# Attention and two feed-forward layers on one core: inverse norm spread by one-pass products, narrower strided scores, and a re-planned order

## The chip, the cores and the metric

The kernel runs on one core of one Trainium2 chip. TensorE, VectorE, ScalarE, GpSimd (POOL in the profile) and SyncE work side by side, each through its own instruction stream, and wait for one another by semaphores; SyncE issues the DMA transfers. The metric is the device time of one execution in microseconds. Before the change the median of three runs is 887.65 us.

## What is computed

Attention over 4 batches, 8 heads, 576 positions and a head width of 64: the first four heads see a local window of 32 positions, the last four every 32nd position. The result, 2304 tokens by 512, goes through a gated feed-forward layer with an RMS norm ahead of it, and then through a second layer with a squared ReLU.

```python
mask_local = (rel >= 0) & (rel < stride)
mask_strided = (rel >= 0) & (pos[None, :] % stride == pos[:, None] % stride)
...
scores = np.where(masks[None, :, :, :], scores, -1000000000.0)
...
return np.matmul(attn, v).astype(np.float32)
```

```python
rms = np.sqrt(np.mean(x * x, axis=-1, keepdims=True) + 1e-06)
xn = x / rms * rms_g
g = xn @ w_gate
silu = g * (1.0 / (1.0 + np.exp(-g)))
val = xn @ w_val
return (silu * val @ w_out).astype(np.float32)
```

```python
h = x @ w_in
r = np.maximum(h, 0.0)
g = r * r
return (g @ w_out).astype(np.float32)
```

## The kernel before

**Attention.** There are 16 units, each a batch with a pair of heads; even units are local, odd units strided. A unit goes through a chain of steps: scores (`att_qk`, products of 64 columns at L476), mask and exponentials, sums, a norm (`att_norm`, L545), a turn of the probabilities so that keys lie on partitions, and the attention product `xo` with v (`att_pv`, L612). In a strided unit the 576 positions are sorted into 32 residues of 18 positions, and a score tile takes a group of three residues (`GR` = 54 positions), so that 54 of its 64 columns belong to the group. Units 0 to 6 put their scores into the bank pair `a` (`first_acc`) and units 7 and 8 into rotating banks `s`; in these nine the mask is added ahead by a product with the mask (L464, `masked`), in the others by VectorE (`att_mask`, L490). Units 0 to 6 are turned by TensorE (`att_turn`, L567) and copied to SBUF (`att_keep`, L579). The others are turned in blocks of 32 by VectorE, and eight DMAs (`att_swap`, L593) move the turned pieces to their place, `pt<-tr`.

**Norm.** The tokens are worked in five blocks, of 512 columns but for the last. For each block, square sums are taken by one-column products (`msb`, L900; for block 0 they are `ms`, L660), VectorE adds the epsilon (`inv`, L906), POOL takes the power (L913), and `prep_bc` (L922) spreads the inverse root over 128 partitions: for each chunk of up to 128 tokens an f32 product whose stationary operand is the column of inverses, broadcast to 128 columns, against an identity. VectorE multiplies x by the spread and by g (`xn`, L939), and x is split into a high part (ScalarE, L958 or L960) and a low part (VectorE or POOL, L970 or L975).

**Feed-forward.** Weights and x are split into f32r pairs, and each block product is three f32r products (`mm3`, L1427 to L1429), in the first phase 512 columns wide: the "wide products" below, into the rotating banks `gv` and the accumulators `a`. The later phases work on 384 columns, with sums of blocks made by VectorE (L1960) and products at L1912 and L2318. The first phase and the attention are interleaved up to about 245 us.

**What sets the order.** The order of all instructions on every engine is fixed when the program is built, by a planner: each `Task` is a chain of steps, each step has alternatives (an engine letter, a planned cost and, for TensorE, a count of records), and `advance()` takes, among the steps that could start first by the planned times, within `TOL`, the one with the earliest due time. Due times come from the leads and from `PRI`; `LOADF`, `BIAS` and the `D_` constants choose between engines; `PV_AHEAD` bounds how many units the scores may run ahead of the attention products. While `warming`, gaps of TensorE are filled with products on a blank tile (`fill()`, L2479). DMAs that leave SyncE's queue stand in the same plan: `lanes.dma` gives the planned landing. The planner's times are only its own; on the chip, order and semaphores alone count. The core of the choice:

```python
e = min(found, key=lambda e: min(f[0] for f in found[e]))
first = min(f[0] for f in found[e])
start, due, _, task, a = min((f for f in found[e] if f[0] <= first + tol), key=lambda f: f[1:3])
...
if e == "T" and warming and start - free["T"] > 2 * FILL:
    fill(int(FILL_OF * (start - free["T"]) / FILL))
emit(task, a)
```

## Time and profile before

| | |
|---|---|
| median of 3 runs | 887.65 us (886.38 to 887.7) |
| profiled execution, its own time | 888.92 us |
| span from first to last instruction in it | 887.1 us |
| mean granted TensorE clock | 0.995 |
| TensorE busy | 873.0 us (98%) |
| TensorE weight loads busy | 817.5 us (92%) |
| VectorE busy | 646.2 us (73%) |
| ScalarE busy | 449.0 us (51%) |
| POOL busy | 69.4 us (8%) |

Times in the profile are microseconds from the span's start. A row of the timeline has the start, the time from there to the end of the last of its instructions, the engine, the line of the kernel, the operation, the tile written and those read, their shapes and how many instructions of the kind follow one another; in brackets the engine's idle time before it and what ended it. One f32 product stands as two records, an f32r product as one. Successive products overlap, so the price of a product is the distance from its start to the next one's start. A busy share of 98% says that the order of TensorE's instructions is the time, and that its waits are few; the granted clock of a stretch tells whether the same instructions ran at 2.4 GHz (1.00) or at 1.2 GHz (0.50).

### The profile page before, as it was taken

Reading aid. Unit: us, or ns where it says so; the run is one execution under the profiler, and the core shown is the slowest. Engines: PE = TensorE matmul, PEld = TensorE weight load, DVE = VectorE, ACT = ScalarE, POOL = GpSimd, SP = SyncE. Lnnn points to the kernel's source line nnn. Section 1 sums busy time; section 2 is a strip of 40 time slices with the busy share of each in tenths; the row PEclk is TensorE's granted clock in tenths of the full one; section 3 lists DMA queues with packets and bytes.
Section 4 is the critical chain, followed back from the end, with each engine's and each line's share of the span. In section 5 each row is a group of like instructions: output and inputs, shape, how many; then the busy total and the mean of one; then the engine's idle time right before and its main releaser. Section 6 shows DMA issues by size and latency. Waiting matters only on the chain.

```text
span 887.1 us, 17217 instructions
## 1 busy us (share of the span) xinstructions
PE 873.0 (98%) x6777; PEld 817.5 (92%) x6782; DVE 646.2 (73%) x1098; ACT 449.0 (51%) x1149; POOL 69.4 (8%) x64
## 2 busy tenths in 40 slices
PE   7999999999999999999999999999999999999998
PEld 4778778878888999999999999999999999999998
DVE  5998877977889875956975876868875456548466
ACT  5986786323312243534543546656565375364462
POOL 0110600100100000000100100001000003002002
PEclk9999999999999999999999999999999999999999
DMA  9865563676694996494488999876799989949714
GB/s 341 273 215 188 169 217 82 212 234 219 232 362 174 341 408 248 171 356 173 161 322 328 377 406 350 333 273 234 287 303 328 375 323 377 298 178 352 241 34 181
DMA packets 77585, 236.79 MB, mean 267 GB/s; under 512 B 7488, under 2 KB 29760, under 8 KB 71616
## 3 DMA queue, kind: packets, MB, share of 16 engines
q1 hardware_dynamic: 77504, 235.70, 73.4%
q8 instruction: 53, 0.87, 0.4%
q14 instruction: 28, 0.23, 0.1%
HBM read 151.91 MB, written 80.48 MB: 262 GB/s over the span
## 4 chain that ended last, share of the span: by engine, by line
PE 85%; DMA 8%; DVE 5%; issue 1%; ACT 1%; SPq 0%; DVEq 0%; ACTq 0%
PE a L1912 15%; PE pg L1912 8%; PE pb L1912 7%; PE gv L1427 6%; PE a L1427 6%; PE a L1428 5%; PE a L1429 5%; PE gv L1429 5%; PE gv L1428 5%; PE a L2318 5%; PE pg L2318 3%; DMA wst_a<-in_w 3%; DMA wi_d<-wst_a 2%; PE pb L2318 2%; DMA wf_d<-wst_a 1%; PE xo L612 1%
## 5 line engine op out<-in xcount | busy, mean ns | idle before, releaser
L1912 PE MATMUL a<-ra 128*128 128x384 f32 x912 | 173.1, 335 | 0.6 <-DVE fb L1960 0.6
L1912 PEld LDWEIGHTS a<-ra 128*128 128x128 f32 x912 | 159.7, 188 | 1.4 <-DVE fb L1960 0.9
L1427 PE MATMUL gv<-ra 128*128 128x512 f32 (+1 forms) x240 | 91.5, 381 | 0.0
L1428 PE MATMUL gv<-ra 128*128 128x512 f32 (+1 forms) x240 | 88.8, 370 | 0.0
L1429 PE MATMUL gv<-ra 128*128 128x512 f32 (+1 forms) x240 | 88.8, 370 | 0.0
L1912 PE MATMUL pg<-ra 128*128 128x384 f32 x426 | 83.4, 336 | 0.7 <-DVE fb L1960 0.7
L1912 PE MATMUL pb<-ra 128*128 128x384 f32 x426 | 83.0, 335 | 0.3 <-DVE fb L1960 0.3
L1912 PEld LDWEIGHTS pg<-ra 128*128 128x128 f32 x426 | 74.8, 188 | 1.2 <-DVE fb L1960 1.0
L1912 PEld LDWEIGHTS pb<-ra 128*128 128x128 f32 x426 | 74.8, 188 | 0.6 <-DVE fb L1960 0.6
L1366 DVE TENSOR_TENSOR wst_a<-fa,wst_a 128x512 fp32r<-128x512 f32 (+1 forms) x76 | 47.9, 632 | 21.6 <-ACT wst_a L1330 19.2
L1427 PEld LDWEIGHTS gv<-ra 128*128 128x128 f32 x240 | 45.5, 190 | 7.9
L1429 PEld LDWEIGHTS gv<-ra 128*128 128x128 f32 x240 | 45.5, 190 | 7.9
L1428 PEld LDWEIGHTS gv<-ra 128*128 128x128 f32 x240 | 45.6, 190 | 6.9
L1330 ACT ACTIVATE wst_a<-fa 128x512 fp32r<-128x512 f32 (+1 forms) x60 | 34.5, 577 | 31.0 <-DMA wi_d<-wst_a 18.9
L1429 PE MATMUL a<-ra,rb 128*128 128x384 f32 x144 | 48.4, 336 | 0.0
L1427 PE MATMUL a<-ra,rb 128*128 128x384 f32 x144 | 48.4, 336 | 0.0
L1428 PE MATMUL a<-ra,rb 128*128 128x384 f32 x144 | 48.4, 336 | 0.0
L1427 PE MATMUL a<-ra 128*128 128x512 f32 (+1 forms) x120 | 45.6, 380 | 0.9 <-ACT pt L579 0.9
L1428 PE MATMUL a<-ra 128*128 128x512 f32 (+1 forms) x120 | 44.9, 374 | 0.0
L1429 PE MATMUL a<-ra 128*128 128x512 f32 (+1 forms) x120 | 44.9, 374 | 0.0
L1514 ACT ACTIVATE fa<-gv 128x512 f32<-128x512 f32 (+1 forms) x18 | 9.5, 527 | 65.5 <-PE gv L1429 65.5
L1199 DVE SCALAR_TENSOR_TENSOR fa<-wst_a,fa 128x1024 int32<-128x1024 int32 x34 | 41.6, 1224 | 1.0
(259 smaller groups left out, 1913.7 us busy)
## 6 DMA issues: line engine op xcount, KB each, us to landing
wst_a<-in_w SPq DMA_DIRECT2D x34, 1024.0 KB, 6.0
ra<-wi_d SPq DMA_DIRECT2D x18, 1792.0 KB, 10.2
wi_d<-wst_a SPq DMA_DIRECT2D x42, 512.0 KB, 4.0
rb<-wf_d SPq DMA_DIRECT2D x16, 1024.0 KB, 7.8
xf_d<-ra SPq DMA_DIRECT2D x21, 768.0 KB, 5.0
ra<-xf_d SPq DMA_DIRECT2D x21, 768.0 KB, 7.1
wo_d<-wst_a SPq DMA_DIRECT2D x14, 512.0 KB, 8.4
wf_d<-wst_a SPq DMA_DIRECT2D x28, 256.0 KB, 7.0
```

The costliest lines, as they stand in the source:

```text
L612: nc.tensor.matmul(out=o, lhsT=v, rhs=rhs, start=True, stop=True)
L1199: nc.vector.scalar_tensor_tensor(out=bits(), in0=word(1), scalar=-0x40000000, in1=bits(), op0=ALU.bitwise_and, op1=ALU.bitwise_or)
L1330: nc.scalar.activation(out=dst, in_=by_form(raw(a, b)), func=ACTF.Copy)
L1366: eng.tensor_tensor(out=x[:, :, 1], in0=by_form(raw(a, b)), in1=x[:, :, 0].bitcast(F32), op=ALU.subtract)
L1427: nc.tensor.matmul(out=o, lhsT=whi, rhs=x_hi, start=first, stop=False)
L1428: nc.tensor.matmul(out=o, lhsT=whi, rhs=x_lo, start=False, stop=False)
L1429: nc.tensor.matmul(out=o, lhsT=wlo, rhs=x_hi, start=False, stop=last)
L1514: nc.scalar.activation(out=tile_t()[:, :n], in_=ps[:, :n], func=ACTF.Silu)
L1912: nc.tensor.matmul(out=o, lhsT=l, rhs=v, start=need is None and k + n == 0, stop=k == 1 and n == 2, skip_group_check=need is not None,)
L2318: nc.tensor.matmul(out=c[role, m]["ap"][:, :SN], lhsT=l, rhs=v, start=need is None and first and i == 0, stop=last and i == 2, skip_group_ ...
```

## The change

There are five parts. Constants of the planner are new. `prep_hi` and `prep_lo` split the inverse into an f32r pair `ih`, the high part by ScalarE and the rest by POOL or VectorE, and `prep_bc` spreads it with two f32r products for each chunk in place of one f32 product. Strided scores with a mask product have `GR` = 54 columns. A rule forces a wide product: after the opening, where a step would make the time since the planned end of the last wide product longer than `SMALL_RUN`, a wide product that could start within `WIDE_IN` is taken first. And the planned landing of turned pieces is `PT_LAG` later.

```diff
--- before.py
+++ after.py
@@ -54,15 +54,15 @@
 
 RING = 9
 
-ATT_LEAD, ATT_STEP = 5.322, 0
-PREP_LEAD = 6.258
-W_LEAD = 0
-X_LEAD = 4.164
+ATT_LEAD, ATT_STEP = 6.027, 0
+PREP_LEAD = 7.671
+W_LEAD = 0.644
+X_LEAD = 4.057
 WARM0 = 10
 
 HOP = 0.15
 DRAIN = 0.12
-TOL = 0.152
+TOL = 0.044
 FILL, FILL_OF, T0, W1_AT = 0.215, 0.85, 5.3, 11.631
 NRAW = 2
 
@@ -76,12 +76,12 @@
 N_QK, N_PV = {"loc": 160, "str": 96}, {"loc": 144, "str": 88}
 QK0, PV0 = {"loc": 1.0, "str": 0.9}, {"loc": 1.25, "str": 0.9}
 
-PRI = {"qk": -3.7, "mask": 12.1, "mx": -12.4, "exp": -0.1, "eps": -0.5, "sum": 15.6, "norm": -1.1, "turn": 3.4, "keep": 12.1, "tr": -1.6,
-       "swap": -2, "pv": -2.7, "out": -1.4, "sq": -3, "ms0": 9.4, "add": -1.3}
-MXP, LOADF, BIAS = 8.164, 0.752, 0.972
-
-D_BUSY, D_COST, D_LATE, D_COST2 = 138.427, 1.084, 343.785, 0.648
-PV_AHEAD = 5
+PRI = {"qk": -2, "mask": 15.3, "mx": -8.6, "exp": -3.6, "eps": 8.4, "sum": 19.5, "norm": 18.3, "turn": -7.3, "keep": 8.7, "tr": -3.7,
+       "swap": 6, "pv": -6, "out": 1.1, "sq": -3.7, "ms0": 11, "add": -2.5}
+MXP, LOADF, BIAS = 11.454, 0.807, 0.253
+
+D_BUSY, D_COST, D_LATE, D_COST2 = 158.279, 1.01, 343.785, 0.648
+PV_AHEAD = 8
 
 
 NM = 7
@@ -108,12 +108,13 @@
     ("P1", 0, 0, "A", None), ("P5", 3, 1, "D", None), ("P6", 4, 2, "A", "s1"), ("P2", 1, 3, "C", "s1"),
     ("P7", 5, 4, "A", "u2"), ("P3", 6, 5, "D", "s5"), ("P4", 2, 6, "A", "c22"),
 ]
-W2_LEAD, X2_LEAD, L2_LEAD = 9.442, -0.326, 6.418
+W2_LEAD, X2_LEAD, L2_LEAD = 9.489, -0.326, 6.418
 X3_LEAD, O_LEAD, H_LEAD = 3.503, -1.055, -0.697
 O_ORDER = [(0, 0), (0, 1), (1, 0), (1, 1), (0, 2), (1, 2), (0, 3), (1, 3)]
 O_ORDER += [(3, 0)] + [(2, j) for j in range(4)] + [(3, j) for j in range(1, 4)]
 O_ORDER += [(p, j) for p in range(4, 7) for j in range(4)]
 W3_LEAD, LOADF2, BIAS2, TOL2 = 16.305, 0.334, 1.147, 0
+SMALL_RUN, WIDE_IN, PT_LAG = 8.246, 0.509, 0.8
 X2_PRI = -0.95
 
 
@@ -157,7 +158,7 @@
 
     def __init__(self):
         self.free = {"T": 0.0, "D": 0.0, "A": 0.0, "P": 0.0, "Q": 0.0, "M": 0.0, "port": 0.0}
-        self.given, self.fetched = 0, 0.0
+        self.given, self.fetched, self.wide_end = 0, 0.0, 0.0
 
     def start(self, e, ready):
         start = max(self.free["D" if e == "X" else e], ready)
@@ -353,6 +354,9 @@
     def transfer(due, ready, cols, fn, allowed=None, early_t=None, run=0):
 
         spawn([Task(due, [(allowed, [[("Q", 0.0)]], lambda _, t: fn(lanes.dma(cols, t, run=run)), early_t)])], ready)
+
+    def is_wide(part):
+        return len(part) > 2 and part[1] > 0.08 * part[2] and part[1] > 1.0
 
     def advance():
 
@@ -400,6 +404,13 @@
             start, _, _, task, a = min(near, key=lambda f: f[1:3])
         if e == "T" and warming and start - free["T"] > 2 * FILL:
             fill(int(FILL_OF * (start - free["T"]) / FILL))
+        if e == "T" and not warming and start + 2 * half - lanes.wide_end > SMALL_RUN:
+
+            wide_ones = [f for f in found["T"] if is_wide(f[3].steps[0][1][f[4]][0]) and f[0] < start + WIDE_IN]
+            if wide_ones:
+                start, _, _, task, a = min(wide_ones, key=lambda f: f[:3])
+        if e == "T" and is_wide(task.steps[0][1][a][0]):
+            lanes.wide_end = start + task.steps[0][1][a][0][1]
         emit(task, a)
         return True
 
@@ -465,6 +476,7 @@
                     out=sc[h][:, 0:64 * nt], lhsT=cst_sb[:, 0:128], rhs=mask_of(u), start=True, stop=False
                 )
         m = 32 if kind(u) == "loc" else 64
+        w = GR if masked and m == 64 else 64
         for t in range(nt):
             for i in range(128 // m):
                 if m == 32:
@@ -474,7 +486,7 @@
                 for h in range(2):
                     r = slice(64 * h, 64 * h + 64)
                     nc.tensor.matmul(
-                        out=sc[h][m * i:m * i + m, 64 * t:64 * t + 64], lhsT=qt[r, c:c + m], rhs=kt[r, c:c + 64],
+                        out=sc[h][m * i:m * i + m, 64 * t:64 * t + w], lhsT=qt[r, c:c + m], rhs=kt[r, c:c + w],
                         start=not masked, stop=not masked or t == nt - 1,
                     )
         for h in range(2):
@@ -746,7 +758,7 @@
             take("pt")
             turn("pt")
             att_swap(u)
-            cell["pt"] = lanes.dma(128 * nt, t, 8, 64 * nt)
+            cell["pt"] = lanes.dma(128 * nt, t, 8, 64 * nt) + PT_LAG
             give("tr", cell["pt"])
 
         def turned(_, t):
@@ -822,7 +834,7 @@
         if u < NM:
             steps += [
                 (
-                    lambda: in_turn("qk", u) and (u < 2 or ("sc", u - 2) in done), [[("T", QK0[kd] + 0.5, N_QK[kd] + 4)]], qk,
+                    lambda: in_turn("qk", u) and (u < 2 or ("sc", u - 2) in done), [[("T", QK0[kd] - (0.1 if kd == "str" else 0.0) + 0.5, N_QK[kd] + 4)]], qk,
                     lambda: max(done["qk", u], done.get(("sc", u - 2), 5.3)), due - 10 - PRI["qk"],
                 ),
                 (
@@ -834,7 +846,7 @@
             steps.append(step(
                 "qk", lambda: in_turn("qk", u) and order.get("prep", 0) and order.get("pv", 0) >= u - PV_AHEAD
                 and room("s", 2) and room("sm") and in_turn("sm", u),
-                [[("T", QK0[kd] + (0.5 if masked else 0.0), N_QK[kd] + (4 if masked else 0))]], qk,
+                [[("T", QK0[kd] + ((0.5 if kd == "loc" else 0.4) if masked else 0.0), N_QK[kd] + (4 if masked else 0))]], qk,
                 lambda: max(done["qk", u], rel["s"][1], rel["sm"][0] - 2.0),
             ))
             if masked:
@@ -914,15 +926,29 @@
             out=inv[:CH, :m], in0=inv[:CH, :m], in1=half[:CH, 0:1].to_broadcast([CH, m]), op=ALU.pow
         )
 
+    def prep_hi(i):
+        inv = pend[i][1]
+        m = len(chunks(i))
+        pend[i] += (st_p.tile([128, 2, 8], F32R, tag="ih", name="ih"),)
+        nc.scalar.activation(out=pend[i][2][:CH, 0, :m], in_=inv[:CH, :m], func=ACTF.Copy)
+
+    def prep_lo(i, eng):
+        _, inv, two = pend[i]
+        m = len(chunks(i))
+        eng.tensor_tensor(
+            out=two[:CH, 1, :m], in0=inv[:CH, :m], in1=two[:CH, 0, :m].bitcast(F32), op=ALU.subtract
+        )
+
     def prep_bc(i):
-        inv = pend[i][1]
+        _, inv, two = pend[i]
         ps = s_p.tile([128, 512], F32, tag="s", name="bc")
         o = 0
         for e, (_, _, skip, m) in enumerate(chunks(i)):
-            nc.tensor.matmul(
-                out=ps[:, o:o + m], lhsT=inv[:CH, e:e + 1].to_broadcast([CH, 128]), rhs=ident[:CH, skip:skip + m],
-                start=True, stop=True,
-            )
+            for h in range(2):
+                nc.tensor.matmul(
+                    out=ps[:, o:o + m], lhsT=two[:CH, h, e:e + 1].to_broadcast([CH, 128]),
+                    rhs=cst_sb[:CH, skip:skip + m], start=h == 0, stop=h == 1,
+                )
             o += m
         pend[i] = ps, inv
 
@@ -1086,8 +1112,10 @@
             ),
             (None, [[("D", 0.2)]], inv, None),
         ]) + [
-            (None, [[("P", 1.1)]], pw, None),
-            (lambda: room("s"), [[("T", 0.25 * nch, 4 * nch)]], bc, lambda: rel["s"][0]),
+            (None, [[("P", 1.25)]], pw, None),
+            (None, [[("A", 0.22)]], lambda _, t: prep_hi(i), None),
+            (None, [[("P", 0.25)], [("X", 0.2)]], lambda p, t: prep_lo(i, nc.gpsimd if p[0][0] == "P" else nc.vector), None),
+            (lambda: room("s"), [[("T", 0.14 * nch, 4 * nch)]], bc, lambda: rel["s"][0]),
         ] + ([(None, [dve(n, True), act(n, True)], keep, None)] if i == 0 else [])))
 
 
```

The order changes from the opening to the end of attention; the tail of TensorE's stream, some 3,700 products, stands in the same order. Three places follow. On TensorE at the square sums and the spread of block 1 (`msb` square sums, `sc` scores of a unit, `bc` the spread, `gv` wide products) the order before is:

```order
L1429 MATMUL gv<-ra 128x512
L900 MATMUL msb<-ones,ssq 128x1 x5
L476 MATMUL sc<-fa 64x64 x24
L922 MATMUL bc<-cst_sb,inv 128x64
L922 MATMUL bc<-cst_sb,inv 128x128 x3
L922 MATMUL bc<-cst_sb,inv 128x64
L1427 MATMUL gv<-ra 128x512
```

and now:

```order
L1457 MATMUL a_1278<-ra 128x512
L912 MATMUL msb<-ones,ssq 128x1 x5
L1455 MATMUL gv<-ra 128x512
...
L488 MATMUL sc<-fa 32x64 x40
L1455 MATMUL gv<-ra 128x512
...
L948 MATMUL bc<-cst_sb,ih 128x64 x2
L948 MATMUL bc<-cst_sb,ih 128x128 x6
L948 MATMUL bc<-cst_sb,ih 128x64 x2
```

Twelve wide products now stand between the square sums and a local score, and twelve more between that and the spread, whose ten products stand in place of five.

On TensorE in the opening, from the turn of unit 3 (`a_179<-cst_sb,sm`) to the turn of unit 4 (`a_178<-cst_sb,sm`), the order before is (`ms` the first block's square sums, `xo` an attention product):

```order
L567 MATMUL a_179<-cst_sb,sm 64x64 x24
L660 MATMUL ms_182<-ones,sq 128x1 x4
L612 MATMUL xo<-pt,v 64x64 x22
L464 MATMUL a_179<-cst_sb 128x384 x2
L476 MATMUL a_179<-fa 64x64 x24
L1427 MATMUL gv<-ra 128x512
...
L922 MATMUL bc<-cst_sb,inv 128x128 x4
L567 MATMUL a_178<-cst_sb,sm 64x64 x20
```

and now, from the attention product of unit 3 to the first wide product behind that of unit 4 and the spread:

```order
L624 MATMUL xo<-pt,v 64x64 x22
L475 MATMUL a_179<-cst_sb 128x384 x2
L488 MATMUL a_179<-fa 64x54 x24
L579 MATMUL a_178<-cst_sb,sm 64x64 x20
L672 MATMUL ms_182<-ones,sq 128x1 x4
L475 MATMUL a_178<-cst_sb 128x320 x2
L488 MATMUL a_178<-fa 32x64 x40
L624 MATMUL xo<-pt,v 64x32 x36
L1455 MATMUL gv<-ra 128x512
...
L948 MATMUL bc<-cst_sb,ih 128x128 x8
```

The wide products that stood between these steps now stand ahead of the turn of unit 3 and behind the attention product of unit 4; the fillers ahead of the first product into a bank `a` of the feed-forward layer are 59 in place of 47.

On SyncE, from the weight stores ahead of unit 14's turned pieces (`pt<-tr 32x320`) to those of unit 15 (`pt<-tr 32x384`, the second), the order before is (`wst` loads of weights, `wi_d` stores of split weights, `yp_d` a 1 MB store of block results, `v` a load):

```order
L1357 DMA wi_d_128<-wst_a 256x1x512
L1140 DMA wst_a<-in_w 128x2x1024
L1357 DMA wi_d_128<-wst_a 256x1x512
L1607 DMA yp_d<-fa 512x1x512
L439 DMA v<-in_strd 128x768
L1357 DMA wi_d_128<-wst_a 256x1x512
L593 DMA pt<-tr 32x320 x8
L1357 DMA wi_d_128<-wst_a 256x1x256
```

and now:

```order
L1385 DMA wi_d_128<-wst_a 256x1x512 x2
L605 DMA pt<-tr 32x320 x8
L1635 DMA yp_d<-fa 512x1x512
L1385 DMA wi_d_128<-wst_a 256x1x512
L1385 DMA wi_d_128<-wst_a 256x1x256
L450 DMA v<-in_strd 128x768
L1168 DMA wst_a<-in_w 128x2x1024
L605 DMA pt<-tr 32x384 x8
```

The store of `yp_d` has moved from ahead of unit 14's pieces to behind them, and so stands between them and unit 15's.

## Rows read from the trace of the kernel before

**Rows 1.** The page's part 1: busy time of each engine.

```profile
PE 873.0 (98%) x6777; PEld 817.5 (92%) x6782; DVE 646.2 (73%) x1098; ACT 449.0 (51%) x1149; POOL 69.4 (8%) x64
```

**Rows 2.** What TensorE waited for, whole span: total us, times, longest.

```profile
PE xo L612 <- issue: 2.9, 1, 2.9
...
PE pg L1912 <- DVE fb L1960: 0.7, 1, 0.7
```

**Rows 3.** Two stretches by engine: length, busy us, granted clock, DMA share, GB/s.

```profile
104.10:107.50 3.40, 3.40 (x13) 3.01 (x13) 3.05 (x9) 3.35 (x20) 3.40 (x5) 0.50 1.02 410
...
199.65:203.05 3.40, 3.40 (x9) 2.63 (x8) 2.14 (x3) 2.03 (x6) 0.00 (x0) 0.50 0.80 225
```

**Rows 4.** TensorE in time, 89 to 107 us: start, us, instruction [idle <-releaser].

```profile
89.10 0.93 PE L476 MATMUL sc<-fa 64*64 64x64 f32 x48
89.96 0.50 PE L1427 MATMUL gv<-ra 128*128 128x512 f32 x1
...
100.31 0.39 PE L1429 MATMUL gv<-ra 128*128 128x512 f32 x1
100.54 1.17 PE L900 MATMUL msb<-ones,ssq 128*128 128x1 f32 x10
101.64 1.25 PE L476 MATMUL sc<-fa 64*64 64x64 f32 x48
103.65 1.97 PE L922 MATMUL bc<-cst_sb,inv 128*128 128x64 f32 x10 [0.76 <-DVE sm L490]
...
105.96 0.63 PE L1428 MATMUL gv<-ra 128*128 128x512 f32 x1
```

**Rows 5.** TensorE in time: a local unit's attention product, and that of unit 14.

```profile
115.96 1.25 PE L612 MATMUL xo<-pt,v 64*64 64x32 f32 x72
117.14 0.50 PE L1427 MATMUL gv<-ra 128*128 128x512 f32 x1
...
196.82 0.30 PE L612 MATMUL xo<-pt,v 64*64 64x32 f32 x4
...
198.30 1.12 PE L612 MATMUL xo<-pt,v 64*64 64x32 f32 x60 [0.38 <-DMA pt<-tr]
199.35 0.56 PE L1427 MATMUL a<-ra 128*128 128x512 f32 x1
```

**Rows 6.** The norm's small tiles, and TensorE around square sums and spread.

```profile
L922 PEld LDWEIGHTS bc<-cst_sb,inv x40: 185/190/333, 45.1 to 234.6; 128*128 128x128 f32 x40
...
L906 DVE TENSOR_SCALAR inv<-msb x4: 151/158/167, 101.8 to 231.6; 128x5 f32<-128x5 f32 x2, 128x4 f32<-128x4 f32 x1, 128x2 f32<-128x2 f32 x1
...
156.85 0.95 PE L900 MATMUL msb<-ones,ssq 128*128 128x1 f32 x8
157.66 0.48 PE L1427 MATMUL gv<-ra 128*128 128x512 f32 x1
...
222.57 1.22 PE L922 MATMUL bc<-cst_sb,inv 128*128 128x128 f32 x10
223.61 0.47 PE L1427 MATMUL gv<-ra 128*128 128x512 f32 x1
```

**Rows 7.** TensorE in time, the opening: fillers, a turn, scores, the bank a.

```profile
8.34 3.88 PE L2479 MATMUL warm<-blank 128*128 128x512 bf16 x17 [0.16 <-issue]
...
35.94 1.61 PE L567 MATMUL a<-cst_sb,sm 64*64 64x64 f32 x48 [0.28 <-DVE sm L545]
...
41.06 0.56 PE L476 MATMUL a<-fa 64*64 64x64 f32 x19 [0.40 <-issue]
...
62.75 0.50 PE L1427 MATMUL a<-ra 128*128 128x512 f32 x1 [0.87 <-ACT pt L579]
```

**Rows 8.** SyncE's DMA queue around unit 14: start, us to issue, transfer.

```profile
183.36 0.59 SPq L1607 DMA_DIRECT2D yp_d<-fa  x1
185.62 0.33 SPq L439 DMA_DIRECT2D v<-in_strd  x1
...
186.77 10.11 SPq L593 DMA_DIRECT2D pt<-tr  x8
```

## The prediction

> **What bounds the kernel now.** I read the page first: TensorE is busy for 873.0 of 887.1 us [rows 1], so the time is TensorE's instruction stream, plus the few places where that stream pauses, plus the places where it runs at half clock. A faster VectorE or ScalarE is worth nothing by itself. The list of what TensorE waited for comes second, and it is short [rows 2]: the longest entry is 2.9 us of "issue", one wait of an attention product in the opening; behind it nothing is over 0.9 us, and of the stages behind the opening only sums at L1960 stand there, with 0.7. Third come the stretches with their granted clock [rows 3]: two of them, 104.10 to 107.50 and 199.65 to 203.05, ran at a granted clock of 0.50, which is 1.2 GHz of 2.4. At half clock 3.4 us do the work of 1.7, so each fall costs **1.7 us**. What stood ahead of a fall is the fourth view, TensorE's instructions in order. Before the first fall come ten square-sum products of one column, 48 small score records, a wait of 0.76 us on the mask add, and the spread of the norm [rows 4]. Before the second, the attention product of unit 14 stops for turned pieces [rows 5]. Both places are narrow work with a wait in it, and both are followed by wide products that take longer: 0.63 us each where one takes 0.39 at full clock [rows 4].
>
> So what this change can win is counted directly: the two falls, the waits ahead of them, and whatever the narrow instructions themselves become cheaper by.
>
> **Part 1: the spread in two one-pass products.** A 512-column block's spread is 10 or 8 records, each with a load of 128 columns. The trace has 40 loads [rows 6]. The new form has two f32r products for each old f32 product, and the old one already stands as two records in the trace, so 40 records stay 40 records. What sets their distance? Eight square-sum records with one column each go from 156.85 to 157.66, 101 ns each, though they stream nothing; ten spread records with up to 128 columns go from 222.57 to 223.61, 104 ns each [rows 6]. The load, not the columns, sets both. I take **0**. The other end: if the columns set it, one pass is priced by a wide product, 230 ns for 512 columns (100.31 to 100.54) [rows 4], in proportion 57 ns at 128. Then 40 x (104 - 57) = 1.9 us would be won. For each of the five blocks ScalarE gets a copy of the inverse and POOL or VectorE a subtraction, both on a few columns; VectorE's own small step on the inverse takes 0.16 us [rows 6]. They lie between the power and the spread, and there the new order has 12 or more wide products in every block but the first, and scores, a turn and six wide products in that, so they are hidden; without that cover they would cost about 0.3 us a block. The Trainium skill, "TensorE: Matmul & The Clock Gate", section "Back-to-back issue gap", gives 81 ns for a sustained pair of load and product of 128 columns; by it the spread would gain 40 x (104 - 81) = 0.9 us, an estimate from that page. The trace's 101 ns at a single column speak against it.
>
> **Part 2: scores of 54 columns.** Four masked strided units write 54 columns instead of 64. A record's price by its columns: an attention product of 72 records with 32 columns takes 1.18 us until the next (115.96 to 117.14), 16.4 ns each [rows 5]; a strided score of 48 with 64 columns takes 0.86 (89.10 to 89.96), 17.9 ns each [rows 4]. Ten columns fewer are 10/32 of that difference, 0.5 ns; by 48 records and 4 units **-0.1 us** (bounds 0, where only the record counts, and -0.5, where a record's 17.9 ns shrink in proportion: 48 x 4 x 17.9 x 10/64 = 0.54).
>
> **Part 3: the opening.** The order has 59 fillers against 47, all ahead of the first product into the bank `a`. A filler takes 0.22 us (17 in 3.88 us) [rows 7], so 12 add 2.6 us unless they fill waits that are there anyway. What can go: the 0.87 us before the first `a` product (the copy of a turned unit by ScalarE), 0.40 us of issue within a score product, and 0.28 before a turn [rows 7], 1.55 together: in the new order 24 wide products stand between that turn and its neighbour, so its copy is covered. The 2.9 us of issue [rows 2] lie ahead of the place where the orders part, and stay. I take 2.6 - 1.55 = **+1.1 us** (bounds -1.5, where fillers only fill waits, and +2.6).
>
> **Part 4: the two falls and their waits.** In block 1 the new order puts 12 wide products, one local score and 12 wide products between square sums and spread. The spread no longer queues on a score bank that the mask has yet to empty, and no narrow stretch is left there. Gone: 1.7 us of clock, and the score's time until the next, 2.01 us (101.64 to 103.65) where the same kind of score takes 0.86 [rows 4], so 1.15. At unit 14 the pieces go out ahead of the 1 MB store of yp instead of behind it: in the trace that store is issued at 183.36 and SP's next issue comes at 185.62, 2.3 us later, while the eight pieces follow at 186.77 and take until 196.88 to be issued [rows 8]. Their planned landing is also 0.8 later. Gone: 1.7 us of clock, and the attention product's 2.53 us (196.82 to 199.35) fall to 1.18 [rows 5], so 1.35. Sum **-5.9 us**.
>
> **Part 5: what comes in their place.** Every step between 63 and 245 us stands somewhere else. I can follow the order, not the waits that it makes. Three places are doubtful: unit 15's pieces are now the ones behind the store, two weight stores and a load; POOL takes some 15 more instructions than before, splits above all; and the new stretch without wide products in the opening (rival 2). The old order lost 5.9 us in the same stretch, in two places. I take half of it, **+2.95 us**; bounds 0 and 5.9. After 245 us the order is the same up to the choice of buffers, so the waits on VectorE's sums at L1960 [rows 2] stay, and cost nothing more or less.
>
> **Sum.** 0 - 0.1 + 1.1 - 5.9 + 2.95 = -1.95 us. The profiled execution took 888.92 us, 1.27 above the median of 887.65 of the runs. 888.92 - 1.95 = 887.0 for a profiled run; **885.7** against the median.
>
> **The rivals.**
> *1. Nothing gained.* New waits of some 5 us in place of 2.95, one of them a fall of 1.7 behind another narrow stretch, bring back all that the repair won: 885.7 + 2.05 is 887.7. For it speaks that the rule that forces a wide product acts by planned times, and the old order, planned in the same way, had them. Against it, that both places are visibly repaired in the order.
> *2. Slower.* The new opening has one stretch with no wide product between the attention products of units 3 and 4: attention, mask, scores, turn, sums, mask, scores, attention, some 250 records in about 7 us by the same steps in the trace of before. In the old opening such a run of small records ended in 2.9 us of issue [rows 2], and two narrow stretches were followed by a fall of 1.7. If both strike, 2.9 + 1.7 = 4.6 us come on top: 890.3. It decides from 3.7 us on, where 885.7 passes 889.4. Against it: behind that one wait the longest for issue in the opening is the 0.40 us of part 3.
> *3. The spread becomes cheap.* The columns set the price and 1.9 us are won: 883.8. For it: the one-pass form isn't in the trace at this width, and all 40 spread records in it are of the f32 form; against it, the 101 ns of records with one column. The page of the Trainium skill that part 1 names has a figure between.
> *4. A clean order.* New waits of about 0.5 us in place of 2.95, and both falls gone: 885.7 - 2.45 is 883.2.
>
> **How the numbers follow.** A measurement of this kernel tells about 0.2%, 1.8 us, from no change: faster is under 885.9, slower over 889.4. My forecast (new waits of 1.5 to 4.3 us, so 884.2 to 887.0) gets 0.40, of which 0.25 is faster and 0.15 the same; rival 1 gets 0.20 (0.18 same, 0.02 slower); rival 2 gets 0.14 (0.13 slower, 0.01 same); rival 3 gets 0.10 and rival 4 gets 0.16, all faster but 0.01. Together 0.50 faster, 0.35 same, 0.15 slower. The range 881.8 to 889.2 leaves out most of rival 2 and the best end of rival 4, where all bounds fall well.
>
> **What would show it.** Right: no stretch after the opening at 0.50 before the end; unit 14's attention product about 1.2 us long with no wait on turned pieces; a spread of about 1.0 us; TensorE's waits between 63 and 245 us of under 3 us together. Wrong: a spread of about 0.6 us (rival 3), a wait of "issue" of over 1 us between 38 and 55 us (rival 2), or a new stretch at 0.50 behind unit 15's attention product or behind a square sum (rival 1). If the first `a` product starts over 3 us later than 62.75, part 3 was priced too low.

## The result and the profile after

The change is **slower**: 896.78 us, the median of four runs (896.26 to 899.72), against 887.67 for the kernel before, measured beside it (886.38 to 887.81). The ratio is 1.0105, with a 95% interval of 1.0085 to 1.0125. The prediction was 885.7 and its range ended at 889.2, so it has the wrong sign. The profiled execution took 899.72 us with a span of 897.89, 10.8 more than the one before [rows 1], so the profile shows the whole loss, and a little more.

The page of after, its busy times and the shares of the chain that ended last:

```profile
PE 876.0 (98%) x6788; PEld 816.9 (91%) x6794; DVE 643.0 (72%) x1079; ACT 457.1 (51%) x1159; POOL 88.8 (10%) x83
...
PE 71%; DMA 15%; DVE 10%; ACT 2%; issue 2%; POOL 0%; SPq 0%; ACTq 0%; DVEq 0%; POOLq 0%
```

TensorE is busy for 3 us more than in [rows 1], POOL for 19 us more. The second line says more than the first: the chain that sets the end now runs on TensorE for only 71% of the time. The same line of the kernel before:

```profile
PE 85%; DMA 8%; DVE 5%; issue 1%; ACT 1%; SPq 0%; DVEq 0%; ACTq 0%
```

The list of what TensorE waited for, after, longest in total first (us in total, times, longest):

```profile
PE xo L624 <- ACT sm L536: 2.3, 2, 1.7
PE xo L624 <- issue: 2.0, 1, 2.0
PE a L1940 <- ACT fa L1966: 1.6, 1, 1.6
PE xo L624 <- DMA pt<-tr: 1.3, 2, 0.8
PE pg L1940 <- DVE fb L1988: 1.3, 2, 0.7
...
PE gv L1456 <- issue: 1.2, 1, 1.2
```

Beside [rows 2] the longest wait on issue is shorter, 2.0 in place of 2.9, but a second one of 1.2 has come. Waits on ScalarE are new: an attention product that waits for a bank which the exponentials still read, and, late in the program, products at L1940 that wait for ScalarE and VectorE.

Where the time went is read off three marks that both traces have: the first product into the bank `a`, the first product of 256 columns (from there on both have the same TensorE instructions in the same order), and the last product.

```
                            before    after
first product into a         62.75    70.28   +7.53
from there to first 256     219.04   216.48   -2.56
from there to the last      601.44   606.78   +5.34
```

The first mark does not hold quite the same work: unit 7's scores stand ahead of it now and stood behind it before. On TensorE they take 1.29 us, after; before, they stood at 69.75 and took 1.30:

```profile
56.01 0.51 PE L475 MATMUL sc<-cst_sb 128*128 128x384 f32 x2
...
57.30 0.50 PE L1455 MATMUL gv<-ra 128*128 128x512 f32 x1
```

So some 6.2 of the 7.53 us are lost in the opening and 1.3 have only moved, and of the 2.56 won behind it 1.3 are those same products.

**The places that the change repaired** look as forecast. The stretches of [rows 3] in the trace of after (length, busy us of PE, PEld, DVE, ACT and POOL, then the granted clock, 1.00 now, DMA share and GB/s), and as a third row the only new one at half clock before the end:

```profile
104.08:107.49 3.41, 3.41 (x18) 2.86 (x18) 3.06 (x9) 2.96 (x10) 2.98 (x4) 1.00 0.30 118
199.65:203.06 3.41, 3.41 (x23) 2.81 (x16) 3.31 (x4) 1.53 (x5) 0.00 (x0) 1.00 1.02 352
...
21.50:28.40 6.90, 6.57 (x122) 5.58 (x119) 5.13 (x6) 4.91 (x23) 1.78 (x1) 0.51 0.80 263
```

The spread of block 1 and the attention product of unit 14, in TensorE's order of time, answer to [rows 4] and [rows 5]:

```profile
103.26 1.20 PE L948 MATMUL bc<-cst_sb,ih 128*128 128x64 f32 x10
104.29 0.47 PE L1455 MATMUL a<-ra 128*128 128x512 f32 x1
...
198.50 1.25 PE L624 MATMUL xo<-pt,v 64*64 64x32 f32 x72
199.68 0.50 PE L1455 MATMUL gv<-ra 128*128 128x512 f32 x1
```

The spread takes 1.03 us to the next product, as in [rows 6] (1.04): one pass saves nothing. Unit 14's product takes 1.18, with no wait. But the wait has come back one unit later. Unit 15's pieces stand behind the store now, and its product stops for them twice, 1.34 us, as much as unit 14's repair was to give (1.35):

```profile
211.72 0.33 PE L624 MATMUL xo<-pt,v 64*64 64x64 f32 x4 [0.84 <-DMA pt<-tr]
212.55 0.81 PE L624 MATMUL xo<-pt,v 64*64 64x64 f32 x40 [0.50 <-DMA pt<-tr]
```

Nor are unit 14's pieces out sooner in this execution. They are issued from 187.50 to 196.82, in [rows 8] from 186.77 to 196.88, and the product comes 1.68 us later than before:

```profile
187.50 9.32 SPq L605 DMA_DIRECT2D pt<-tr  x8
```

**The opening** is where the prediction broke. VectorE's norms of units 3, 5 and 6, before:

```profile
34.93 0.96 DVE L545 TENSOR_TENSOR sm<-sm,ri 128x768 f32<-128x768 f32 x1
...
52.95 0.96 DVE L545 TENSOR_TENSOR sm<-sm,ri 128x768 f32<-128x768 f32 x1
58.60 0.82 DVE L545 TENSOR_TENSOR sm<-sm,ri 128x640 f32<-128x640 f32 x1
```

and after:

```profile
38.60 1.80 DVE L557 TENSOR_TENSOR sm<-sm,ri 128x768 f32<-128x768 f32 x1
...
55.79 0.96 DVE L557 TENSOR_TENSOR sm<-sm,ri 128x768 f32<-128x768 f32 x1
63.78 1.08 DVE L557 TENSOR_TENSOR sm<-sm,ri 128x640 f32<-128x640 f32 x1
```

A norm ends a unit's chain of scores, maximum, exponentials and sums, and TensorE's turn waits for it. The 7.53 us are three steps of this chain: unit 5's norm is 2.84 later (55.79 against 52.95); from it to unit 6's 7.99 pass in place of 5.65, 2.34 more; and from that to the first product into `a` 6.50 in place of 4.15 [rows 7], 2.35 more. Ahead of unit 3's norm, 3.67 late, lies the stretch at half clock from 21.6, half of whose length is 3.4. It is not what makes `a` late: in the run of the change's order with the old forms, below, nothing ahead of `a` is at half clock, and the three steps are 1.52, 2.39 and 2.35, 6.26 together. The second step holds unit 7's scores, ahead of unit 5's turn. What fills the last step is seen on TensorE, after:

```profile
65.42 1.32 PE L579 MATMUL a<-cst_sb,sm 64*64 64x64 f32 x37
...
68.58 0.81 PE L624 MATMUL xo<-pt,v 64*64 64x64 f32 x40 [1.67 <-ACT sm L536]
70.28 0.50 PE L1455 MATMUL a<-ra 128*128 128x512 f32 x1 [0.89 <-ACT pt L591]
```

and on ScalarE in the same microseconds:

```profile
65.70 0.35 ACT L536 ACTIVATE sm<-sc,nm 128x64 f32<-128x64 f32 x1
...
66.81 1.13 ACT L1209 ACTIVATE fa<-wst_a 128x1024 f32<-128x1024 f32 x1
67.85 0.29 ACT L536 ACTIVATE sm<-sc,nm 128x64 f32<-128x64 f32 x1
...
69.46 0.77 ACT L591 ACTIVATE pt<-a 128x320 f32<-128x320 f32 x2
```

The exponentials on `sc` are unit 7's, which the new order gives out before unit 5's attention product and unit 6's copies. They hold the banks that unit 5's product wants (1.67), a step of the weights (1.13) stands among them, and the copy that frees `a` comes only at 69.46, though the turn ended before 67. In the trace of before, unit 7's scores come after the first product into `a`.

### The profile page after: what moved, and what is told of

Its sections match the earlier page's. It is cut to its first block, busy times and chain, and to the rows that moved or that the text cites. A ratio compares the mean times of both kernels' runs of the same rounds, so it can differ in the third digit from the quotient of the medians.

```text
span 897.9 us, 17241 instructions
## 1 busy us (share of the span) xinstructions
PE 876.0 (98%) x6788; PEld 816.9 (91%) x6794; DVE 643.0 (72%) x1079; ACT 457.1 (51%) x1159; POOL 88.8 (10%) x83
## 4 chain that ended last, share of the span: by engine, by line
PE 71%; DMA 15%; DVE 10%; ACT 2%; issue 2%; POOL 0%; SPq 0%; ACTq 0%; DVEq 0%; POOLq 0%
PE a L1940 14%; DMA wi_d<-wst_a 9%; PE pg L1940 8%; PE pb L1940 7%; PE a L2346 5%; PE a L1455 4%; PE a L1456 4%; PE a L1457 4%; DMA wst_a<-in_w 3%; PE pg L2346 3%; PE gv L1455 3%; PE gv L1456 3%; PE gv L1457 3%; DMA wf_d<-wst_a 2%; PE pb L2346 2%
## 5 line engine op out<-in xcount | busy, mean ns | idle before, releaser
L1940 PE MATMUL a<-ra 128*128 128x384 f32 x912 | 173.4, 335 | 2.5 <-ACT fa L1966 1.6
L1940 PEld LDWEIGHTS a<-ra 128*128 128x128 f32 x912 | 159.7, 188 | 3.8 <-ACT fa L1966 1.9
L1940 PE MATMUL pg<-ra 128*128 128x384 f32 x426 | 83.7, 336 | 1.9 <-DVE fb L1988 1.3
L1940 PE MATMUL pb<-ra 128*128 128x384 f32 x426 | 83.2, 335 | 1.3 <-DVE fb L1988 1.2
L1940 PEld LDWEIGHTS pg<-ra 128*128 128x128 f32 x426 | 74.6, 188 | 3.1 <-DVE fb L1988 2.2
L1940 PEld LDWEIGHTS pb<-ra 128*128 128x128 f32 x426 | 74.8, 188 | 1.9 <-DVE fb L1988 1.9
L1394 DVE TENSOR_TENSOR wst_a<-fa,wst_a 128x512 fp32r<-128x512 f32 (+1 forms) x73 | 45.7, 628 | 29.5 <-ACT wst_a L1358 28.6
L1394 POOL TENSOR_TENSOR wst_a<-fa,wst_a 128x512 fp32r<-128x512 f32 (+1 forms) x13 | 17.4, 1341 | 342.4 <-ACT wst_a L1358 341.9
L1455 PE MATMUL a<-ra 128*128 128x512 f32 (+1 forms) x120 | 45.1, 376 | 0.9 <-ACT pt L591 0.9
L1456 PE MATMUL a<-ra 128*128 128x512 f32 (+1 forms) x120 | 44.2, 369 | 0.0
L1457 PE MATMUL a<-ra 128*128 128x512 f32 (+1 forms) x120 | 44.2, 368 | 0.0
```

What stands on the lines that cost most here:

```text
L1394: eng.tensor_tensor(out=x[:, :, 1], in0=by_form(raw(a, b)), in1=x[:, :, 0].bitcast(F32), op=ALU.subtract)
L1455: nc.tensor.matmul(out=o, lhsT=whi, rhs=x_hi, start=first, stop=False)
L1456: nc.tensor.matmul(out=o, lhsT=whi, rhs=x_lo, start=False, stop=False)
L1457: nc.tensor.matmul(out=o, lhsT=wlo, rhs=x_hi, start=False, stop=last)
L1940: nc.tensor.matmul(out=o, lhsT=l, rhs=v, start=need is None and k + n == 0, stop=k == 1 and n == 2, skip_group_check=need is not None,)
```

## The experiments

Where an experiment moves steps and no code, its diff lists the order in which the steps are given out, one step of one unit on a line.

### The two new forms apart from the order

**Both forms in the old order.** Edit, from the kernel before: `prep_hi`, `prep_lo` and the one-pass `prep_bc` as in the change, and the 54 columns; the constants stay.

> The order of before, step by step, with only the two new forms put in: the one-pass spread (a copy and a subtraction more in front of it) and 54 columns. Theory A (the loss is the opening's new order): no change, 886 to 888, first product into the bank a within 0.5 us of 62.75. Rival B (the new forms cost time through the copy and the subtraction in front of the spread): 890 or more.

Measured: 891.87 us, ratio 1.0055 [1.0036, 1.0075]. TensorE at block 1 in this trace:

```profile
101.04 1.25 PE L486 MATMUL sc<-fa 64*64 64x64 f32 x48
104.45 1.64 PE L948 MATMUL bc<-cst_sb,ih 128*128 128x64 f32 x10 [2.16 <-DVE sm L500]
...
106.47 0.63 PE L1454 MATMUL gv<-ra 128*128 128x512 f32 x1
```

From score to spread 3.41 us pass where [rows 4] have 2.01. The extra steps on ScalarE and VectorE lie bare where no wide products cover them. The spread waits for VectorE's mask add, which empties its bank, and VectorE does the subtraction first, five columns in 0.98 us beside a step on POOL, behind a wait of 0.40 for ScalarE's copy:

```profile
102.55 2.50 POOL L1248 TENSOR_TENSOR ra<-fa,ra 128x512 fp32r<-128x512 f32 x2
102.85 0.98 DVE L937 TENSOR_TENSOR ih<-inv,ih 128x5 fp32r<-128x5 f32 x1 [0.40 <-ACT ih L932]
103.76 1.01 DVE L500 SCALAR_TENSOR_TENSOR sm<-sc,cst_sb 128x384 f32<-128x384 f32 x2
```

That is 1.4 us, far over the 0.3 that the prediction named for a block without cover. Falls at 105.2 and 200.8 are in this trace too; what else the 5 us hold is not settled.

**The columns alone.**

```diff
+        w = GR if masked and m == 64 else 64
-                        out=sc[h][..., 64 * t:64 * t + 64], ..., rhs=kt[r, c:c + 64],
+                        out=sc[h][..., 64 * t:64 * t + w], ..., rhs=kt[r, c:c + w],
```

> The kernel before with the strided masked scores 54 columns wide and nothing else; every instruction is in its old place. Theory (the columns are worth about 0.1 us, and the 5 us that both forms cost together come from the uncovered split of the spread in block 1): a ratio of 0.999 to 1.001. Rival (the narrower score moves the loss): 1.003 or more.

Measured: 886.87 us, 0.999 [0.9973, 1.0008]. The columns are worth nothing that can be told, so the loss of the run above is the spread's. This run has a second use, since every instruction stands where it stood in the kernel before. Its trace shows the places of both falls [rows 3] at full clock, with the same wait and the same broken product of unit 14 ahead of them. TensorE in time, then the two stretches by engine and clock:

```profile
102.61 1.30 PE L923 MATMUL bc<-cst_sb,inv 128*128 128x64 f32 x10 [0.77 <-DVE sm L491]
...
195.56 1.12 PE L613 MATMUL xo<-pt,v 64*64 64x32 f32 x60 [0.37 <-DMA pt<-tr]
```

```profile
102.50:106.50 4.00, 3.90 (x22) 3.46 (x23) 3.82 (x10) 4.00 (x24) 4.00 (x5) 1.00 1.02 407
196.00:201.00 5.00, 5.00 (x63) 4.23 (x57) 3.14 (x5) 2.04 (x6) 0.00 (x0) 1.00 0.90 250
```

**The order alone.** Edit, from the change: the old f32 spread and 64 columns; `prep_hi` and `prep_lo` stay as planned times and issue nothing, so that the order is the change's.

> The order of the change, step by step, with the old forms: f32 spread without the copy and the subtraction, 64 columns. Theory A: as slow as the change, 895 to 898, first product into the bank a at about 70. Rival B: near before, 887 to 890.

Measured: 899.39 us, 1.0124 [1.0081, 1.0166]; first product into `a` at 69.01, with no half clock ahead of it. The order makes the whole loss. Of the constants that set it, `SMALL_RUN` and `WIDE_IN` have no part: with their rule left out, the same order comes out on every engine, so here the rule forces nothing.

### Is it the opening?

**The change's order up to 117 us, the old order behind it**, and **the reverse**; both with the old forms.

```diff
 order of steps, joined at unit 8's attention product
-before: opening to unit 8 | rest
+new head: the change's opening to unit 8 | rest of before
+old head: before's opening to unit 8 | rest of the change
```

> Old forms; the change's order up to the attention product of unit 8 (near 117 us), the order of before behind it. Theory (the opening alone makes most of the loss): first product into a at 68.5 to 71 and 893 to 896 us in all, 5 to 8 over the kernel before, with the stretch behind 245 us as long as before, 643.3 to 644.5. Rival (a late start is won back, since VectorE and ScalarE have done work of unit 7 ahead of time): under 890 us.

> The reverse, with old forms: the order of before up to the attention product of unit 8, the change's order behind it. Theory: first product into a at 62 to 64.6, the stretch up to 245 us at least as short as before's, and the 2 to 3 us behind it that every execution of the change's order lost: 886 to 889 us. Rival (the loss is made by what the change does behind 117 us): 892 us or more.

Measured: the new head 893.82 us, 1.0070 [1.0045, 1.0094], first product into `a` at 71.62. The opening alone loses 6 us, as the theory said. The old head 892.74, 1.0057 [1.0037, 1.0077], over the 886 to 889 expected: the theory is only half right. Its trace shows no such loss in the opening (62.33), but the joint has waits of its own, such as an attention product at 121.9 that stops 1.7 us for turned pieces. How much of the 4.9 us is the joint's and how much the change's is not settled. In this trace the move on SyncE does what part 4 said: unit 14's pieces are issued by 191.19, ahead of the store, and its product starts at 193.83 with no wait; unit 15's has none either.

**A part of the opening given out by the old priorities.** Edit: the old `PRI`, `MXP`, `LOADF`, `BIAS`, `TOL` and `D_COST` until 60 us, for the first seven units.

> All of the change, but units 0 to 6 keep the old table of priorities and the planner the old constants up to 60 us of planned time, so that the opening stands in the order of before up to the first spread. Theory A: first product into the bank a at 62 to 64, and the time 883 to 888, since what the change repairs behind the opening stays. Rival C (about half of the loss comes from waits behind 245 us, whatever the opening does): 889 to 892.

Measured: 897.91 us, 1.0117 [1.0085, 1.0149]; first product into `a` at 71.24. A miss: unit 7's scores still came early, at 56.6.

### Which part of the opening?

**The fillers.** The new head without the 13 and 5 fillers ahead of unit 3's turn and product.

```diff
-fill 13
 u3 TensorE turn
-fill 5
 u3 TensorE attention product
```

> As the run of the new head, without the 13 and the 5 fillers ahead of unit 3's turn and attention product. Theory F (the fillers themselves, 18 of 0.22 us, hold TensorE up): the first product into a comes 2 to 4 us sooner than with them, and the time falls as much. Theory A (ScalarE's and VectorE's queues set it; the fillers only fill waits): the first product into a comes within 1 us of the new head's, the gaps show as waits on VectorE's norm or ScalarE, and the time stays within 1.5 us, or rises by a fall of the clock.

Measured: 893.96 us, 1.0063 [1.0044, 1.0081]; with them it was 893.82. The turn of unit 3 now waits in the fillers' place, and the norm ahead of it is again a long one, 1.78 us:

```profile
36.13 0.40 PE L1525 MATMUL gv<-ra 128*128 128x512 f32 x1
38.88 1.61 PE L663 MATMUL a<-cst_sb,sm 64*64 64x64 f32 x48 [2.35 <-DVE sm L641]
```

18 fillers of 0.22 us are 4 us of TensorE and cost nothing that the medians tell: they filled a wait on VectorE. The first product into `a` came at 67.92, 3.7 us sooner, in an execution with 1.7 us of half clock ahead of it where the new head's own had 5.1; against the order alone, which had none, it came 1.1 sooner.

**Unit 7, both ways.** First in the old order:

```diff
 u6 TensorE scores
+u7 TensorE scores, VectorE maximum, ScalarE exponentials
 u5 TensorE attention product
 u6 ScalarE copies, first product into a
-u7 TensorE scores, VectorE maximum, ScalarE exponentials
```

> The kernel before, with only unit 7's scores, maximum and exponentials moved ahead of unit 5's attention product, as they stand in the change. Theory A: the kernel before gets the change's late start, the first product into a at 65 to 67 in place of 62.75, unit 5's attention product above 3 us in place of 1.74, and the time rises by 2.5 to 4 us, a ratio of 1.003 to 1.0045. Rival B: first product within 1 us of 62.75, ratio within 1.001.

Measured: 889.81 us, 1.0020 [1.0003, 1.0037]; first product into `a` at 65.53. VectorE's norms of units 5 and 6:

```profile
53.54 0.96 DVE L641 TENSOR_TENSOR sm<-sm,ri 128x768 f32<-128x768 f32 x1
61.64 0.82 DVE L641 TENSOR_TENSOR sm<-sm,ri 128x640 f32<-128x640 f32 x1
```

8.10 us apart in place of 5.65: the second step of the chain, made in the kernel before by this move alone. The third step is not there: from unit 6's norm to `a` 3.89 pass, before 4.15. The start of `a` is 2.8 late, the time 1.8, a little under the 2.5 expected; 1.3 of the 2.8 are unit 7's scores, which have only moved ahead of the mark. Then in the change's order the reverse, unit 7 behind unit 6's copies and unit 5's product ahead:

> The change's own order, but unit 7's scores, maximum and exponentials come behind unit 6's copies, and unit 5's attention product ahead of them. Theory A (the opening is bound by ScalarE, and it does unit 7's work, 12 rows and 3.3 us, too early): the first product into a comes at 66 to 67.5 in place of 70.28, unit 5's attention product takes 1.7 to 2 in place of 3.65, and the time falls by 2 to 4 us against the change, so the ratio to the kernel before is 1.006 to 1.008. Rival B (it is TensorE's fillers and the norms on VectorE that set the opening): the first product into a stays within 1 us of 70.28 and the ratio at 1.010.

Measured: 902.55 us, 1.0165 [1.0146, 1.0185]. A miss in time: the first product into `a` came at 68.33, 2 us sooner beside the same 3.4 us of half clock, so the mark moves with unit 7 both ways. But a bank was then late for the next score:

```profile
PE sc L570 <- ACT xr L753: 4.2, 1, 4.2
```

**ScalarE's order.** The change without the 18 fillers, unit 3's exponentials ahead of unit 2's copies and square, two weight steps behind them; on TensorE unit 3's turn comes ahead of the six wide products before it.

```diff
+u3 ScalarE exponentials
 u2 ScalarE copies, square
-u3 ScalarE exponentials
-ScalarE weight steps
-fill 13, fill 5
 u3 TensorE turn, attention product
+ScalarE weight steps
```

> The change, without the 18 fillers ahead of unit 3's turn and attention product; on ScalarE unit 3's exponentials come ahead of unit 2's copies and square, and two weight steps stand behind unit 3's. Theory A (ScalarE's order makes the late start): unit 3's attention product begins at 39 to 41 in place of 43.66, the first product into a at 65 to 67.5 in place of 70.28, and 892 to 894.5 us in all, against 896.8 for the change. Rival (the total of ScalarE's and VectorE's work sets it, whatever the order): the first product into a at 69 or later, the time within 1.5 us of the change.

Measured: 897.07 us, 1.0108 [1.0073, 1.0144]; first product into `a` at 68.69. In time the rival holds, though its mark was 69 or later. Unit 3's norm starts at 35.71, 2.9 us sooner than in the change, and 1.6 of that are left at `a`. The same edit with the fillers left in had given:

> The order of the change, but ScalarE does the exponentials of unit 3 without a break, ahead of the outputs and squares of unit 2's attention product (as in before), and six to eight steps that hang on these come behind the turn of unit 3. Theory E (ScalarE's order delays the turn of unit 3): the turn comes at 38 to 39 instead of 40.92, the first product into a at 67 to 68.5, the time 2 to 3 us less. Rival: the chain behind (unit 7's early scores) sets the first product into a whatever the turn does, 70 to 71.

Measured: 901.16 us, 1.0156 [1.0123, 1.019]. Unit 3's norm is early here too, at 35.84, and the first product into `a` late, at 72.79: a miss for both. Four fillers more behind unit 1's turn, against the stretch at half clock from 21.6:

> The order of the change with four fillers more behind the turn of unit 1, where the granted clock fell to 0.50 at 21.59 us. Theory D (the fall behind the narrow stretch at 17 to 22 us delays the opening): the fall is shorter or gone, and the first product into the bank a comes at 68.5 to 69.5 instead of 70.28, the time 1 us less. Rival E (ScalarE's queue sets the opening, TensorE's clock is hidden): first product into a at 70 to 71, the time unchanged or 1 us more.

Measured: 897.72 us, 1.0117 [1.0093, 1.0140]. The stretch moved to 32.4 and grew to 10.2 us, and the first product into `a` came at 73.68, later than either expected. Unit 7 late, ScalarE's order and these four together:

> The order of the change with three mends in its opening: the four fillers; unit 3's exponentials without a break; and the scores of unit 7 moved behind the turn of unit 6, with unit 5's attention product, its outputs and unit 6's copies ahead of them. Theory A (the opening holds the loss, in three places): first product into a at 64 to 66 and the time 4 to 6 us less than the change, 890 to 893 where the change has 897. Rival F (some of the loss comes from behind 245 us): first product into a at 64 to 66, but the time above 894.

Measured: 906.75 us, 1.0217 [1.0169, 1.0264], with five stretches at half clock up to 94 us and the first product into `a` at 74.16, where 64 to 66 was expected.

The executions side by side, in us; half clock is what stretches at 0.50 ahead of the first product into `a` cost at most, half of their length there:

```
                     first a   half clock   a to 256   256 to last
before                 62.75      0           219.0       601.4
 54 columns            61.69      0           217.0       601.0
 forms alone           62.17      1.7         220.7       602.0
 unit 7 early          65.53      0           214.7       601.8
 old head              62.33      1.7         219.3       602.5
 units 14, 15 later    63.55      1.7         215.3       602.3
after                  70.28      3.4         216.5       606.8
 order alone           69.01      0           216.7       602.1
 new head              71.62      5.1         217.0       602.1
  without fillers      67.92      1.7         215.8       602.1
 unit 7 late           68.33      3.4         226.7       605.9
 ScalarE first         68.69      3.8         218.9       602.4
 POOL steps back       69.26      2.0         218.0       603.9
```

The first column does not follow the second. With no half clock ahead of it the order alone is still 6.26 us late, and with 1.7 us of it the forms alone and the old head are not late at all.

### Behind 245 us

**POOL's steps.** The change gives POOL 27 steps that VectorE did before. They are given back, each in its place.

```diff
-27 steps on POOL (weight steps, splits, norms)
+the same 27 on VectorE
```

> The change's own order; the 27 steps that POOL does in it and VectorE did before are back on VectorE, each at its place in the order. TensorE, ScalarE and SyncE have the same instructions in the same order. Theory G (VectorE runs slower while POOL works beside it, so a sum or norm beside such a step comes late): the wait of 0.8 us on VectorE's sum near 365 us is gone, the sum there takes 0.95 in place of 1.69, and the time falls by 1 to 3 us, a ratio of 1.007 to 1.009. Rival H (VectorE, at 72% busy, is delayed more by the 27 steps than by POOL beside it): same time or slower, a ratio of 1.010 or more.

Measured: 896.67 us, 1.0101 [1.0080, 1.0121], as the change. The mechanism is there. After, a step on POOL at 363.83 (first row) and VectorE beside it (the second, 1.69 us); last, from the trace of before, the same step of VectorE without POOL, 0.95:

```profile
363.83 1.30 POOL L1394 TENSOR_TENSOR wst_a<-fa,wst_a 128x512 fp32r<-128x512 f32 x1 [123.25 <-ACT wst_a L1358]
```

```profile
364.26 1.69 DVE L1768 TENSOR_TENSOR fb<-fb 128x768 f32<-128x768 f32 x1
```

```profile
356.62 0.95 DVE L1740 TENSOR_TENSOR fb<-fb 128x768 f32<-128x768 f32 x1
```

With the step back on VectorE it is 0.95 again, and TensorE's wait for the step behind it, 0.64 us ahead of 366.47, is gone. But another wait grew (1.58 in place of 1.16 near 530), the way from `a` to the 256 columns took 1.5 us more, and by the medians nothing is won. The same on the old head:

> As the run of the old head, and the steps behind the joint that POOL does in the change and VectorE did before are back on VectorE, each at its place. Theory G (POOL beside VectorE slows VectorE's sums): the waits of 0.8 us near 357 us and of about 0.5 near 488 us are gone, and it is 1 to 2.5 us faster than the old head alone. Rival: within 0.7 us of it, since the waits behind 480 us do not come from those steps.

Measured: 894.46 us, 1.0057 [1.0034, 1.0080]; the rival holds here as well.

**No lag for the turned pieces.** `PT_LAG` 0.8 to 0.0, in the change.

> The change without the 0.8 us on the planned landing of turned pieces; the order parts from the change's at the square sums of block 2 only. Theory A: the opening as in the change (first product into the bank a at about 70), the time within 2 us of it, 894 to 899; more waits of attention products on turned pieces than in the change. If the lag itself costs the time: under 892.

Measured: 916.78 us, 1.0335 [1.0301, 1.0369]. The lag shifts the planned order of everything behind it, weights too: a product waits 15.6 us for `rb`. The run says nothing of the pieces themselves.

### The repairs without the rest

**Both places repaired in the kernel before**: block 1's score stands behind twelve of the wide products; the attention products of units 14 and 15 and block 3's square sums and spread come twelve wide products later. SyncE's queue stays.

> The order and the forms of before, with the two places mended that the prediction counted at 5.9 us: in block 1 twelve wide products between square sums and score and twelve between score and spread; the attention products of units 14 and 15, the square sums and the spread behind them each behind twelve more wide products. If part 4 of the prediction was right: no stretch at 0.50 between 95 and 215 us, the time 4 to 6 us less than before. Rival: the falls and waits come back in other places, the time within 2 us of before.

Measured: 895.75 us, 1.0095 [1.0070, 1.0120]. TensorE waits 3.8, 1.9 and 1.0 us for VectorE and POOL, whose queues stood as before, and a stretch at half clock stands at 118.6, so neither the expectation nor its rival holds. **Only the units:**

```diff
-u14 TensorE attention product
 12 wide products
+u14 TensorE attention product
 (u15's product, block 3's square sums and spread in the same way)
```

> The kernel before, with its old forms; only the pieces of units 14 and 15 go out ahead of the 1 MB store, as in the change, and block 3's square sums and spread move as they do there. Block 1 stays as it was, so its fall near 104 stays. Theory (this part of the change is worth what the prediction gave it, 1.7 of clock and 1.35 of the attention product): no stretch at 0.50 between 190 and 215 us, and 2 to 3 us less than the kernel before, a ratio of 0.9966 to 0.998. Rival: the queues of VectorE, POOL and SyncE hand the wait to another place, and the ratio lies within 0.999 to 1.002.

The edit is not the one that this expectation tells. The queues of SyncE, VectorE, ScalarE and POOL are those of the kernel before, and the pieces still follow the store:

```profile
183.35 0.60 SPq L1702 DMA_DIRECT2D yp_d<-fa  x1
...
186.52 9.45 SPq L688 DMA_DIRECT2D pt<-tr  x8
```

Only TensorE's order moved, and it covers the wait with twelve wide products.

Measured: 885.51 us, 0.9978 [0.9959, 0.9997], against 888.02 for the kernel before beside it. Unit 14's product, to the next 1.18:

```profile
198.52 1.25 PE L707 MATMUL xo<-pt,v 64*64 64x32 f32 x72
199.70 0.50 PE L1522 MATMUL gv<-ra 128*128 128x512 f32 x1
```

The ratio is just clear of 1. This version is the only one faster than the kernel before, and it is no part of the change: it mends unit 14 without the move on SyncE. That move by itself, in the kernel before, was not run.

## Why the prediction was wrong

**Part 1 and rival 3: right on the price, too low where nothing covers.** The spread takes 1.03 us after and 1.04 before, so one pass saves nothing; the Trainium skill's 81 ns a pair ("TensorE: Matmul & The Clock Gate", section "Back-to-back issue gap") is not reached in either form. "About 0.3 us a block" without cover was too little: 1.4 in block 1 of the forms alone. In the change the two steps are covered but for one wait of 0.4.

**Part 2: right.** 0.999 alone.

**Part 3, the step that failed.** "I take 2.6 - 1.55 = +1.1 us" stands where 7.53 were measured, or 6.2 without unit 7's scores, outside its bounds of -1.5 and +2.6. It priced TensorE's fillers and TensorE's own short waits, and put the order of VectorE and ScalarE at nothing. The run without fillers shows no price for them, and the 0.87 that was to go ahead of the first `a` product is still there, 0.89. The new head shows that the opening's order costs 6 us, and the runs of unit 7 that its place in the chain through VectorE and ScalarE makes 2.0 to 2.8 of the late start; the rest of that chain was not taken apart. The error lies ahead of part 3: "a faster VectorE or ScalarE is worth nothing by itself" left those two engines out, and in the first 63 us TensorE's turns and attention products wait for them. A table of windows for the opening gives the sign, here of before (length, busy us of PE, PEld, DVE, ACT and POOL, clock, DMA share and GB/s):

```profile
16.00:38.60 22.60, 18.18 (x539) 14.69 (x525) 20.59 (x32) 18.51 (x79) 3.56 (x2) 1.00 0.84 292
38.60:62.75 24.15, 22.88 (x482) 19.16 (x481) 21.87 (x36) 21.68 (x88) 3.93 (x3) 1.00 0.74 247
```

VectorE is busy for 20.59 of 22.60 and 21.87 of 24.15, ScalarE for 18.51 and 21.68, while the page's 73% and 51% [rows 1] are means over stages in which they idle. TensorE is as busy, 22.88 of 24.15 in the second window, so the shares do not name the engine that sets the pace; the times of the norms do. Work put ahead of need on an engine with so little slack delays what is needed.

**Part 4: the places right, the price wrong.** Unit 14's wait is gone, and 1.34 of its 1.35 us have come back at unit 15. Covering the wait by another edit gives 2.5 us by the medians. The two falls, 3.4 of the 5.9 us, are in the profiled execution of before and not in that of the 54 columns, which has the same order. The prediction set its sum against one execution, 1.27 us over the median, and took both falls as lasting.

**Part 5: the net between 63 and 245 us too good, the end wrong.** Without part 3 the forecast for that stretch was -0.1 - 5.9 + 2.95 = -3.05; measured to the first 256-column product -2.56, and without unit 7's scores, which had moved ahead of it, some -1.3. So what came in place of the 5.9 is nearer 4.7 than 2.95, inside the bounds, and that the two sums lie close is luck. "After 245 us ... cost nothing more or less" failed: 5.34 us in the profiled execution, 0.7 to 4.5 in the others of the change's order above against 601.4; executions of the old order have up to 602.3. TensorE's order is the same there, but the steps of VectorE, POOL and ScalarE that feed it are not: its waits there add up to 5.5 us after and 1.6 before. Which of them cost what is open: giving POOL's steps back mended one wait of 0.64 and no more that the medians tell.

**Rival 2 had the sign**, 890.3 at 0.14: a narrow opening, a wait and a fall. The place was another in the main. Between the products of units 3 and 4 nothing new waits long; the fall is at 21.6 and the longest new wait at unit 5's product, at 66.9. But its sign came, a wait of "issue" of over 1 us between 38 and 55:

```profile
54.88 0.39 PE L1456 MATMUL gv<-ra 128*128 128x512 f32 x1 [1.16 <-issue]
```

Two more of the prediction's signs came: the first `a` product over 3 us late, and TensorE's waits between 63 and 245 us, 5.6 in place of under 3.

**What stays open.** The parts add up by the ratios, 6.2 for the head and 5.1 for the rest against 11.0 for the order alone, but the joints have waits of their own, and the interval of the order alone is wide, 7 to 15 us. So only the 6 of the opening are shown. Of those, unit 7's place is 1.8 by its own run. The rest is argued to be the earlier chain; no single edit gave it back, and each moved a wait to the next queue. That the half clock adds to it is not shown.

## What to carry to other kernels

Look at each stage's own windows before calling an engine idle: one that is at 51% of a span can be at 90% of the stage that a change reorders, and there the time comes from its queue. Price a moved step on every engine that it uses, and follow one unit's chain (score, maximum, exponentials, norm, turn, product) in the new order; one unit's scores, maximum and exponentials given out early cost more here than 18 fillers. Compare two orders at marks, and count whether the same work stands ahead of each mark. Before you count the repair of a fall of the clock as a gain, see whether it is there in a second execution.

## What the runs showed of the hardware

The granted clock falls at the same program point in one execution and not in another: with the same instructions but for 54 columns, and the same waits ahead, 104.10 to 107.50 ran at 0.50 before [rows 3], and its counterpart at 1.00 with the 54 columns. The forms alone had both falls again, the run of unit 7 early neither.

VectorE steps with two inputs slow down beside POOL: 1.69 us in place of 0.95, and unit 3's norm 1.80 in place of 0.96, both while POOL works. The Trainium skill says so ("GPSIMD Engine Reference", section "1. Specifications": contention with VectorE instructions with two SBUF inputs), and the trace agrees; the price, 0.7 to 0.8 us a step, is the trace's. With POOL's steps back on VectorE the two took 0.95 us each.
